# Weight sums on GpSimd, 512-column steps and another order of issue in a fused attention and feed-forward kernel

## The chip, the cores and the metric

The kernel runs on one core of a Trainium2 chip. The metric is the device time of one execution in microseconds. A core has five engines that each run their own instructions in order and wait for each other by semaphores: TensorE (PE in the profile; PEld is its weight load), VectorE (DVE), ScalarE (ACT), GpSimd (POOL) and SyncE (SP), which issues the DMAs here.

## The reference

Four batches of 768 positions with 8 heads of 64 go through chunked attention: each chunk of 32 queries sees 8 memory keys, 16 keys to its left, its own 32 and 8 to its right. The result, 3072 tokens of width 512, goes through a feed-forward layer of width 2048.

```python
for c in range(nc):
    ...
    scores = scale * np.matmul(q_c, k_full.transpose(0, 1, 3, 2))
    scores = scores - np.max(scores, axis=-1, keepdims=True)
    a = np.exp(scores)
    a = a / (np.sum(a, axis=-1, keepdims=True) + 1e-09)
    out[:, :, c_start:c_end] = np.matmul(a, v_full)
...
h = x @ w_in
g = np.where(pos, h, np.where(neg, 0.0, (h + beta) ** 2 / (4.0 * beta)))
return (g @ w_out)
```

## The kernel before, in words

The 3072 tokens are six blocks of 512 (`TB`), each of two halves of 256. The width of 2048 is 16 column groups of 128 (`NFC`), counted by `fc` from 0. Every float32 factor of the feed-forward layer is split into a high part and a low part, and a product is three matmuls: high x high, high x low and low x high.

The program has two parts.

**Blocks 0 and 1.** Generators of small pieces of work are advanced one piece at a time, in the order that the string `FIRST` (line 27) writes out. A name there is one piece, a `+` is the next load of the list `early` (line 811).
- `g0` to `g3` are the attention of block 0 (line 253); `n0`, `n1` are that of block 1's halves, `n2`, `n3` that of block 2 (line 410): scores on PE, softmax on DVE and ACT, six transposes on DVE into `pt`, values on PE, then the high and low parts `xth` and `xtl`.
- `w0` to `w15` decode a piece of the weights (line 189) that a DMA brought as `w`: a scaling on ACT, three bit operations on DVE into `f`, the high part on ACT and the low part on DVE, both into `wr`. Piece i holds the first layer's weights of group i + 1 and the second layer's of group i - 1, but for the ends.
- `A`, `B`, `C`, `D` with a group's number are a `half_step` (line 443) on one half of 256 tokens: `A` and `B` on the halves of block 0, `C` and `D` on those of block 1. It has 12 matmuls of 256 columns into a bank of `ps_h` (two banks), three activations on ACT into `gw` and `gt`, a join on DVE into `gw`, the high part `gh` on ACT, the low part `gl` on DVE, and 6 matmuls of 512 columns into `ps_o`. Two half steps share each of the buffers `gw`, `gt`, `gh`, `gl`.
- `t0` to `t7` are a `build` (line 536), one for every two groups of the first layer's weights. It makes what the second part needs: `fef` is high plus low (two sums of 512 columns), `tf` four differences of 256 columns, all six on DVE. Then ACT casts `tf` into the high half of `st`, DVE makes the low half, and SP stores `st` to DRAM as `saved`. `st` has one buffer; `fef`, `tf`, the decode's `f` and the output's `ob` share two buffers of one tag.

**Blocks 2 to 5.** Here the first layer is computed with seven products in place of eight, on sums of the weights (`saved`, loaded back into freed places of the weights, `load_t`, line 564) and on sums of the tokens. Four strings `QUADS` (line 66) give the order of work within a block, a quarter of the groups each: `p` is a product of 12 matmuls of 256 columns into one of the two `ps_h` banks, `c`, `a`, `r`, `m`, `h`, `l` are the copies, additions, activations, joins and splits behind it, `g` the 12 matmuls of 512 columns of an output, digits and `@` advance the attention of the next block. A `-` means the quarter before. The last pieces of block 1 are left over for the first of these quarters (`left`, line 787, `left_store`, line 792). `begin_second` (line 723) issues the first loads of `saved` on SP.

The class `InOrder` (line 86) keeps every engine's instructions in the order in which the code issues them; its line 94 is the line that the profile shows for nearly all of them.

Of the kernel before, what the change touches and what calls it, by code (L numbers as in the profile page):

```python
# [32 lines left out]
    A4 w10 + A4 B3 w5 B4 A5 w11 w6 + B4 w6 A4 w7 w7 B4 A5 B5 B4 w12 + A5 w6 B4 A5 B5 A5 w7 w13 A6 +
    B5 w7 w8 A5 w8 B5 A6 B6 B5 w14 A6 w7 A6 B5 B6 A6 w8 w15 A7 B6 w8 w9 A6 w9 B6 A7 B6 B7 A7 w8 A7
    B6 B7 A7 w9 A8 B7 w9 w10 w10 A7 B7 A8 B7 B8 A8 w9 A8 B7 A8 B8 w10 A9 B8 w10 w11 w11 B8 A8 A9 B8
    A9 B9 w10 A9 A9 B8 w11 B9 B9 A10 w11 w12 w12 B9 A9 A10 B9 w11 B10 A10 w12 A10 B9 B10 A10 w12
    w13 A11 B10 w13 B10 A10 A11 B10 w12 n0 A11 w13 A11 B11 + n0 w13 B10 A11 B11 n0 A12 B11 n0 w13
    B11 A11 A12 n0 B12 n0 n0 B11 n0 B11 B12 A12 n0 A12 A13 A12 n0 n0 A12 A13 w14 n0 B13 w14 n0 A14
# [10 lines left out]
    C11 D12 C10 n3 n3 C11 C12 n3 n3 D12 C12 D12 n3 n3 D12 + C11 n3 D13 n3 C11 D11 D13 C11 n3 D12 n3
    C12 D12 C12 D13 D13 D13 n3 C12 C13 + n3 n3 n3 C13 C12 D14 C13 D14 D13 D14 D14 C14 D14 C13 D15  # L50
    C14 C13 C14 C15 D15 C14 C14 D15 C15 D15 C15 C13 D15 C15 C15
# [48 lines left out]
def attn_ffn_kernel(ctx: ExitStack, tc: tile.TileContext, first_qk, first_v, qk, vw, w, out):  # L100
# [342 lines left out]
    def half_step(blk, half, fc):  # L443
# [41 lines left out]
        ob = apool.tile([P, 2, DM], F32, name="ob", tag="f", bufs=2)  # L485
        for t, copy in enumerate((dve.tensor_copy, act.copy)):
            copy(ob[:, t], acc[blk][2 * half + t])
            r0 = blk * TB + (2 * half + t) * P
            sp.dma_start(out[r0 : r0 + P, :], ob[:, t])
            yield  # L490
# [448 lines left out]
```

## Time and profile before

| what | value |
| --- | --- |
| median of three runs | 609.87 us (609.29 to 611.09) |
| the profiled execution's own time | 609.82 us |
| its span, first to last instruction | 608.0 us |
| PE busy | 583.4 us, 96% |
| PE weight loads busy | 518.6 us, 85% |
| DVE busy | 402.0 us, 66% |
| ACT busy | 344.8 us, 57% |
| POOL busy | 0.7 us |
| granted TensorE clock, mean | 0.994 |

A busy time is the time in which at least one instruction of the engine runs. A row of a timeline has start, length, engine, line, operation, tiles written and read, and in brackets the idle time ahead of it with what ended it. A row of a group has the number of instructions behind an x, the busy time, the mean of one in ns, and the idle time ahead. The part with 40 slices gives the busy share of each fortieth of the span in tenths.

### The profile page before, as it was taken

The page shows a single profiled execution, that of the slowest core. Times are in us where ns is not written, and L with a number is a line of the kernel's source. Part 1 is how long each engine was busy: PE and PEld are TensorE (multiplying, and loading weights), DVE is VectorE, ACT ScalarE, POOL GpSimd, SP SyncE. Part 2 cuts the span into 40 slices and gives each one's busy share as a digit, 9 for nine tenths or more (in the row PEclk, how much of TensorE's full clock was granted, in tenths as well). Part 3 has the DMA queues.
Part 4 walks back from the last instruction along what each step waited for, and adds up shares of the span by engine and source line. Part 5 has one row for each costly group of instructions (what it writes and reads, how often), then busy time and mean ns, then how long its engine had stood idle before and what let it go on. Part 6 is the DMA issues. An engine that isn't in the chain of part 4 may idle for free.

```text
span 608.0 us, 14641 instructions
## 1 busy us (share of the span) xinstructions
PE 583.4 (96%) x6360; PEld 518.6 (85%) x6360; DVE 402.0 (66%) x643; ACT 344.8 (57%) x683; POOL 0.7 (0%) x6
## 2 busy tenths in 40 slices
...
DVE  5799999997899575755557655556655557423332
...
GB/s 354 423 418 419 15 1 106 85 109 192 138 140 248 237 79 237 208 164 150 139 72 114 199 124 189 140 71 106 208 110 101 138 2 5 204 104 46 130 1 70
DMA packets 39441, 91.13 MB, mean 150 GB/s; under 512 B 2896, under 2 KB 29776, under 8 KB 33744
## 3 DMA queue, kind: packets, MB, share of 16 engines
...
q10 hardware_dynamic: 144, 0.13, 0.1%
q14 instruction: 15, 0.12, 0.1%
...
## 4 chain that ended last, share of the span: by engine, by line
PE 74%; DVE 20%; issue 2%; ACT 2%; DMA 1%; DVEq 0%
PE ps_o L94 36%; PE ps_h L94 32%; DVE f L94 5%; PE ps_x L94 3%; PE ps_s L94 2%; DVE pt L94 2%; DVE wr L94 2%; DVE gw L94 2%; DVE pr L94 2%; DVE gl L94 2%; DVE den L94 1%; DVE st L94 1%; DVE mx L94 1%; DVE tf L94 1%; DMA qk<-in_first_qk_dram 1%
## 5 line engine op out<-in xcount | busy, mean ns | idle before, releaser
L94 PE MATMUL ps_o<-wr,gh 128*128 128x512 f32 x768 | 242.3, 397 | 2.0 <-DVE ob L94 1.6
L94 PEld LDWEIGHTS ps_o<-wr,gh 128*128 128x128 f32 x768 | 137.9, 189 | 28.7 <-DVE ob L94 2.4
L94 PE MATMUL ps_o<-wr,gl 128*128 128x512 f32 x384 | 151.6, 395 | 0.1
L94 PE MATMUL ps_h<-xth,wr 128*128 128x256 f32 x512 | 104.4, 291 | 5.5 <-ACT gt L94 5.2
L94 PE MATMUL ps_h<-s,wr 128*128 128x256 f32 x768 | 98.1, 282 | 0.0
L94 PEld LDWEIGHTS ps_h<-s,wr 128*128 128x128 f32 x768 | 95.5, 188 | 1.9
L94 PEld LDWEIGHTS ps_h<-xth,wr 128*128 128x128 f32 x512 | 85.3, 195 | 8.5 <-ACT gt L94 5.8
L94 ACT CAST gh<-gw 128x256 fp32r<-128x256 f32 (+1 forms) x128 | 65.1, 514 | 46.1 <-DVE gw L94 46.1
L94 DVE SCALAR_TENSOR_TENSOR gw<-gw,gt 128x256 f32<-128x256 f32 (+1 forms) x112 | 59.6, 535 | 43.5 <-ACT gw L94 43.0
L94 PEld LDWEIGHTS ps_o<-wr,gl 128*128 128x128 f32 x384 | 72.3, 188 | 17.8 <-DVE gl L94 1.0
L94 DVE TENSOR_TENSOR gl<-gw,gh 128x256 fp32r<-128x256 f32 (+1 forms) x128 | 70.2, 553 | 14.7 <-ACT gh L94 13.3
L94 PE MATMUL ps_h<-xtl,wr 128*128 128x256 f32 x256 | 66.3, 289 | 0.6 <-DVE xtl L94 0.6
L94 ACT ACTIVATE gw<-gw 128x256 f32<-128x256 f32 (+1 forms) x128 | 66.6, 521 | 0.0
L94 DVE TENSOR_TENSOR gt<-gt,ps_h 128x512 f32<-128x512 f32 x32 | 21.9, 686 | 53.9 <-ACT gt L94 43.2
L94 PEld LDWEIGHTS ps_h<-xtl,wr 128*128 128x128 f32 x256 | 50.2, 196 | 2.5 <-DVE xtl L94 0.8
L94 ACT ACTIVATE gw<-ps_h 128x256 f32<-128x256 f32 (+1 forms) x80 | 34.1, 426 | 31.5 <-PE ps_h L94 29.4
L94 PEld LDWEIGHTS ps_h<-sa,wr 128*128 128x128 f32 x384 | 47.9, 188 | 1.4
L94 PE MATMUL ps_h<-sa,wr 128*128 128x256 f32 x384 | 48.8, 282 | 0.0
L94 ACT ACTIVATE gw<-gt 128x512 f32<-128x512 f32 x32 | 20.3, 633 | 46.4 <-DVE gt L94 46.4
L94 DVE STREAM_TRANSPOSE pt<-pr 32x512 f32<-32x512 f32 (+1 forms) x60 | 41.6, 700 | 1.3
L94 DVE SCALAR_TENSOR_TENSOR f<-w,f 128x1024 uint32<-128x1024 uint32 x32 | 39.1, 1221 | 0.4
L94 ACT COPY gt<-ps_h 128x512 f32<-128x512 f32 x32 | 18.8, 587 | 35.2 <-PE ps_h L94 34.8
...
## 6 DMA issues: line engine op xcount, KB each, us to landing
...
w<-in_w_dram SPq DMA_DIRECT2D x16, 1024.0 KB, 19.8
...
v<-in_vw_dram SPq DMA_DIRECT2D x10, 1024.0 KB, 5.6
saved<-st SPq DMA_DIRECT2D x8, 1024.0 KB, 3.9
...
```

The source lines that it names most:

```text
L94: return self.tc.keep_in_program_order(getattr(self.engine, name)(*args, **kwargs))
```

## The change

Three things change.

1. A new generator `step` takes the place of two half steps from the fifth column group on (`fc` 4 to 15), in both blocks: `E` for block 0, `F` for block 1. It works on 512 tokens at once: 12 matmuls of 512 columns into `ps_h`, and one instruction of 512 columns where two half steps had one of 256 each. The 12 matmuls of the second layer are issued in two pieces of 6. Groups 0 to 3 stay half steps.
2. The six sums of a `build` are issued on GpSimd instead of VectorE. The cast on ACT, the low half on DVE and the store stay.
3. `FIRST` and the four strings `QUADS` are written in another order. What is left over for the second part are now the ends of `F14` and `F15`; it is the same number of matmuls.

```diff
-    + g0 w0 g1 w1 g2 + g2 g1 g0 g3 g2 + g1 g2 A0 + g3 g3 g2 g2 g3 g2 A1 A0 + g3 w2 g3 g3 g3 g2 w1
+    + g0 w0 g1 w1 g2 + g2 g1 g0 g3 g2 + g1 g2 A0 + g3 g2 g2 g3 g2 g3 A1 A0 + g2 g2 + g3 g3 w1 A1 w2
...
-LAST = 4
...
-                pe.matmul(to, a[:, ts], m, start=fc == 0 and i == 0, stop=fc == NFC - 1 and i == 2)
+                pe.matmul(to, a[:, ts], m, start=fc == 0 and i == 0, stop=False)
...
+    def step(blk, fc):
+
+        xh, xl = xts[blk]
+        hp = ps_h.tile([P, 512], F32, name="ps_h")
+        wh, wl = weights(0, fc, 0), weights(0, fc, 1)
+        terms = [(wh, x, cc) for cc in range(NP) for x in (xh, xl)] + [(wl, xh, cc) for cc in range(NP)]
+        for i, (m, x, cc) in enumerate(terms):
+            pe.matmul(hp, m[:, cc * P : (cc + 1) * P], x[:, cc], start=i == 0, stop=i == len(terms) - 1)
+        yield
+        g = gpool.tile([P, TB], F32, name="gw", tag="gw")
+        t = gpool.tile([P, TB], F32, name="gt")
+        act.activation(g, hp, AF.Relu, bias=0.5, scale=0.5)
+        act.activation(t, hp, AF.Relu, bias=-1.0)
+        act.activation(g, g, AF.Square)
+        yield
+        dve.scalar_tensor_tensor(g, g, 1.0, t, op0=ALU.min, op1=ALU.add)
+        yield
+        gh = gpool.tile([P, TB], F32R, name="gh", bufs=4)
+        act.copy(gh, g)
+        yield
+        gl = gpool.tile([P, TB], F32R, name="gl", bufs=4)
+        dve.tensor_tensor(gl, g, gh.bitcast(F32), op=ALU.subtract)
+        yield
+        wh, wl = weights(1, fc, 0), weights(1, fc, 1)
+        for half in range(2):
+            for t in range(2 * half, 2 * half + 2):
+                ts = slice(t * P, (t + 1) * P)
+                for i, (a, m) in enumerate(((gh, wh), (gh, wl), (gl, wh))):
+                    pe.matmul(acc[blk][t], a[:, ts], m, start=False, stop=fc == NFC - 1 and i == 2)
+            yield
...
-            dve.tensor_tensor(fef[:, j].rearrange("p a b -> p (a b)"), hi, lo, op=ALU.add)
+            pool.tensor_tensor(fef[:, j].rearrange("p a b -> p (a b)"), hi, lo, op=ALU.add)
...
-        dve.tensor_tensor(tf[:, 1], b12, b11, op=ALU.subtract)
+        pool.tensor_tensor(tf[:, 1], b12, b11, op=ALU.subtract)
...
     def left(which):
-        two = {"22": (0, 2), "21": (2, 4), "12": (4, 4)}[which]
-        for blk, half, fc in items[len(items) - LAST :][slice(*two)]:
-            next(chains[f"{'ABCD'[2 * blk + half]}{fc}"], None)
+        for name in {"22": (2, 2), "21": (1, 1), "12": ()}[which]:
+            next(chains[f"F{NFC - name}"], None)
...
+        "E": lambda fc: step(0, fc),
+        "F": lambda fc: step(1, fc),
```

**Where the sums stood.** The first place is the end of block 1's weight builds. On DVE before, the sums `fef` and `tf` stand between the softmax of an attention (`den`, `rin`, `pr`) and the low parts `gl` and `st`:

```order
L94 TENSOR_TENSOR st<-tf,st 128x4x256
L94 TENSOR_TENSOR fef<-wr_1173 128x512
L94 TENSOR_REDUCE den<-pr 128x16
L94 TENSOR_TENSOR tf<-fef 128x256 x2
L94 TENSOR_TENSOR tf<-fef,tf 128x256
L94 TENSOR_SCALAR den<-den 128x16
L94 TENSOR_TENSOR gl<-gw,gh 128x256
L94 TENSOR_TENSOR tf<-fef,tf 128x256
L94 RECIPROCAL rin<-den 128x16
L94 TENSOR_TENSOR fef<-wr_1295 128x512
L94 TENSOR_TENSOR pr<-pr,rin 128x1024
L94 TENSOR_TENSOR st<-tf,st 128x4x256
```

The same stretch on DVE now, from one low half `st` to the next:

```order
L89 TENSOR_TENSOR st<-tf,st 128x4x256
L89 TENSOR_TENSOR pr<-ps_s,mx 128x1024
L89 TENSOR_TENSOR gl<-gw,gh 128x512
L89 SCALAR_TENSOR_TENSOR gw<-gw,gt 128x512
L89 TENSOR_REDUCE den<-pr 128x16
L89 TENSOR_TENSOR st<-tf,st 128x4x256
```

And POOL now, where nothing but the sums of one build after the other stands there (the sixth and the seventh):

```order
L89 TENSOR_TENSOR fef<-wr_907 128x512
L89 TENSOR_TENSOR fef<-wr_958 128x512
L89 TENSOR_TENSOR tf<-fef 128x256 x2
L89 TENSOR_TENSOR tf<-fef,tf 128x256 x2
L89 TENSOR_TENSOR fef<-wr_978 128x512
L89 TENSOR_TENSOR fef<-wr_1042 128x512
```

The sums have moved from DVE to POOL, and DVE's rows for the activations are 512 columns wide in place of 256.

**What ACT does between two casts into `st`.** The second place is ACT at the same builds. Before, from the sixth cast to the seventh and the activations behind it:

```order
L94 CAST st<-tf 128x4x256
L94 CAST gh<-gw 128x256
L94 ACTIVATE pr<-pr 128x1024
L94 CAST gh<-gw 128x256
L94 CAST st<-tf 128x4x256
L94 ACTIVATE gw<-ps_h 128x256
L94 ACTIVATE gt<-ps_h 128x256
L94 ACTIVATE gw<-gw 128x256
```

Now, from the sixth cast to the seventh and the activations behind it:

```order
L89 CAST st<-tf 128x4x256
L89 ACTIVATE gw<-ps_h 128x512
L89 ACTIVATE gt<-ps_h 128x512
L89 ACTIVATE gw<-gw 128x512
L89 CAST gh<-gw 128x512
L89 CAST st<-tf 128x4x256
L89 ACTIVATE gw<-ps_h 128x512
L89 ACTIVATE gt<-ps_h 128x512
L89 ACTIVATE gw<-gw 128x512
```

A whole step's activations, which read a `ps_h` bank, have come between the two casts; before there was none.

**The decode beside the attention.** The third place is DVE in block 0, where the first attention half of block 1 (`pr`, `pt`) meets the decode of the 15th piece of weights (`w_847` before, `w_814` now). Before:

```order
L94 TENSOR_TENSOR pr<-pr,rin 128x1024
L94 SCALAR_TENSOR_TENSOR gw<-gw,gt 128x256
L94 STREAM_TRANSPOSE pt<-pr 128x512
L94 TENSOR_TENSOR gl<-gw,gh 128x256
L94 STREAM_TRANSPOSE pt<-pr 128x512
L94 STREAM_TRANSPOSE pt<-pr 32x512
L94 TENSOR_SCALAR f<-w_847 128x1024
L94 STREAM_TRANSPOSE pt<-pr 32x512
L94 SCALAR_TENSOR_TENSOR f<-w_847,f 128x1024
L94 STREAM_TRANSPOSE pt<-pr 32x512 x2
L94 SCALAR_TENSOR_TENSOR gw<-gw,gt 128x256
L94 SCALAR_TENSOR_TENSOR f<-w_847,f 128x1024
```

Now:

```order
L89 TENSOR_TENSOR pr<-pr,rin 128x1024
L89 STREAM_TRANSPOSE pt<-pr 128x512 x2
L89 STREAM_TRANSPOSE pt<-pr 32x512 x4
L89 SCALAR_TENSOR_TENSOR f<-w_814,f 128x1024
L89 TENSOR_SCALAR f<-w_859 128x1024
L89 SCALAR_TENSOR_TENSOR gw<-gw,gt 128x512
L89 SCALAR_TENSOR_TENSOR f<-w_814,f 128x1024
L89 TENSOR_TENSOR xtl<-ps_x,xth 128x4x2x64
L89 SCALAR_TENSOR_TENSOR f<-w_859,f 128x1024
L89 TENSOR_TENSOR xtl<-ps_x,xth 128x4x2x64
L89 TENSOR_TENSOR gl<-gw,gh 128x512
L89 TENSOR_TENSOR wr_1322<-f,wr_1322 128x1024
```

The six transposes now stand in one row, ahead of the two combining operations on the 15th piece, and the decode of the 16th piece (`w_859`) has begun among them.

More of the change, by code (lines that the diff above doesn't have):

```diff
@@ L33 @@
[L33 to L38, printed above, removed]
@@ L49 @@
[L49 to L51 removed]
+    + g0 w0 g1 w1 g2 + g2 g1 g0 g3 g2 + g1 g2 A0 + g3 g2 g2 g3 g2 g3 A1 A0 + g2 g2 + g3 g3 w1 A1 w2
+    g3 w1 w3 A0 g3 g2 w2 g3 + g3 w1 w2 g2 + g3 g3 g2 A0 g3 B0 w1 w2 w1 w4 A0 B0 w3 A1 B0 w2 + A2 B1
+    A1 A2 B1 w2 A1 w3 A0 B1 B2 + w5 w3 B1 A2 B0 B0 B2 B1 w3 w4 A3 B2 + w3 A2 w7 A2 w4 B0 w5 A1 B2
@@ new lines @@
+    A2 w6 w4 w5 B3 A3 B2 w4 + B1 B2 w4 E4 + A3 B3 + w8 w6 + w9 A3 w5 w5 A3 w6 w10 B3 w11 w6 w5 w7
+    B3 A3 + E4 + w6 B3 E5 E4 E5 E4 w13 w7 B3 w6 w7 E4 w8 w7 w12 + E6 E5 E4 E4 E7 E5 w8 w14 + E6 E5
+    E5 E5 w7 w15 w8 w9 E6 w8 w9 E6 E6 E7 w9 E6 E7 w8 w9 E6 w9 E7 E7 E8 w10 E8 E9 w11 w10 w10 E8 w10
+    E8 w11 E9 E7 E8 w11 w10 w11 E8 E9 E9 E8 w12 w12 w11 E9 E10 E10 E11 w12 E7 w13 E10 w12 E10 w13 +
+    n0 E10 + E11 w12 E12 E10 E12 E10 n0 w14 w13 w13 n0 E11 n0 E9 w13 E9 E11 n0 E11 n0 E11 n0 n0 +
@@ new lines @@
+    n0 E13 n0 n0 n0 n0 E11 n0 w14 n0 E13 w15 E12 n0 w14 n0 w15 E12 n0 E14 E12 w14 E14 n1 w14 w15
+    E12 w15 n1 E15 E13 n1 E14 E13 n1 E14 E13 n1 C0 E12 n1 w15 n1 E14 n1 C0 n1 n1 n1 E15 E13 n1 C1
+    E15 E13 n1 E15 E14 C1 n1 E15 C1 C2 + C0 C2 C0 C2 C1 n1 C1 E14 n1 C0 n1 E15 n1 C2 E15 C0 E15 E15
+    D0 E15 C1 D1 C3 E15 t0 D0 t0 t0 t0 D3 D0 D1 t0 C2 C3 D1 D0 D1 t0 t0 t1 D0 C3 D0 C3 t0 C3 t1 t1
+    D2 F4 D1 t1 D3 D2 t1 t1 D3 t1 t2 C2 D1 D2 D2 C3 D3 F5 F4 t2 t2 t2 t1 t2 D2 D2 t2 D3 F6 F4 F4 t2
+    t2 F5 F5 t3 t3 t3 F4 t3 t3 F5 D3 F6 F5 F6 F5 t3 t4 F6 t3 t3 t4 F5 t4 F7 t4 n2 t4 F4 t4 t5 t5 F7
@@ L52 @@
+    F4 t4 F7 n2 F6 t5 t5 t4 n2 F8 F7 t5 F7 F9 t5 F8 n2 F8 F6 t6 n2 t6 t6 t5 t6 F6 F9 F8 F7 t5 t6 F8
+    F9 n2 t6 t7 F7 n2 + n2 n2 F11 n2 t6 t7 t6 t7 n2 t7 t7 n2 F10 n2 F11 F9 F9 n2 F10 t7 F10 F12 t7
+    F8 n2 t7 + n2 F10 F8 F10 F11 F11 n3 F13 n3 F9 n2 n3 F12 F10 n3 F11 F12 + F10 n3 n3 F12 F9 n3 n2
+    n3 n3 F11 F13 n3 n3 n3 F12 F11 F14 F13 F14 n3 F12 F12 F13 n3 n3 F15 n3 + F14 F13 n3 F15 F15 F15
+    F13 F15 F14 F14 F13 n3
 """
-LAST = 4
 PROD = {
@@ L67 @@
     """
-    @S0 p2 p1 c1 -h12 -l12 -g22 a11 0 dS4 r11 p6 c2 m11 0 p5 h11 -g12 kS4 0 p7 z0 -g21 0 c3 a22 r22
-    0 z1 l11 0 m22 h22 p3 p4 r21 a12 r12 l22 m21 m12 g11 h21 l21
-    """,
-    """
-    0 0 -h12 p1 p2 0 c1 -g21 0 -l12 a11 0 r11 m11 -g22 p6 c2 h11 0 p5 p7 0 @V0 c3 a22 r22 0 -g12
-    m22 h22 p4 l11 p3 a12 r21 l22 @S1 m21 r12 m12 h21 l21 g11
-    """,
-    """
-    p1 -h12 1 p2 c1 1 a11 r11 1 -l12 m11 -g21 -g22 p6 1 c2 p5 1 p7 c3 a22 h11 -g12 r22 m22 l11 1 p4
-    h22 l22 r21 1 p3 g11 m21 h21 1 a12 1 1 l21 r12 m12 1
-    """,
-    """
-    -g22 p1 1 -h12 c1 p2 -l12 p6 a11 r11 1 kA11 m11 -g21 @V1 c2 1 p7 h11 kA12 l11 dS3 c3 p5 a22
-    -g12 dS1 r22 dS2 p4 p3 m22 h22 g11 l22 a12 r21 kA22 r12 m21 h21 m12 kS1 l21 kS2 kS3
+    @S0 p1 p2 -h12 -g22 c1 p6 a11 p5 0 dS4 r11 0 m11 -l12 0 -g12 c2 kS4 p7 -g21 c3 0 a22 r22 z0 h11
+    z1 0 0 m22 h22 l11 p4 p3 r21 0 a12 l22 r12 g11 m21 h21 l21 m12
+    """,
+    """
+    0 p2 -h12 0 p1 c1 a11 -g21 p6 -l12 r11 m11 0 0 c2 h11 -g22 p7 p5 0 0 c3 a22 @V0 r22 -g12 p4 p3
+    0 m22 h22 l22 l11 r21 a12 r12 @S1 g11 m21 h21 l21 m12
+    """,
+    """
+    1 1 p2 p1 -g22 c1 a11 r11 1 p6 m11 1 1 -h12 p5 -g21 c2 p7 -l12 c3 h11 -g12 a22 l11 r22 m22 1 1
+    h22 p4 l22 r21 p3 1 g11 m21 h21 1 a12 r12 m12 1 1 l21
+    """,
+    """
+    p1 1 -h12 -g22 c1 p2 p6 -g21 a11 c2 -l12 1 kA11 @V1 r11 p7 1 c3 m11 h11 kA12 p5 dS3 a22 -g12
+    dS1 r22 dS2 p4 p3 l11 m22 h22 l22 kA22 a12 r21 g11 m21 r12 kS2 kS1 h21 m12 l21 kS3
     """,
@@ L483, in half_step @@
         if fc < NFC - 1:
             return
[L485 to L490, printed above, removed]
+        for half in range(2):
+            ob = apool.tile([P, 2, DM], F32, name="ob", tag="f", bufs=2)
+            for t, copy in enumerate((dve.tensor_copy, act.copy)):
+                copy(ob[:, t], acc[blk][2 * half + t])
+                r0 = blk * TB + (2 * half + t) * P
+                sp.dma_start(out[r0 : r0 + P, :], ob[:, t])
+                yield
```

23 lines of the change are left out of this document (5 added, 18 removed).

## The prediction

> **What bounds the kernel now.** I read the page first, then busy time by stretch, then the engines' timelines where TensorE (PE) stands idle. The page:
>
> ```profile
> span 608.0 us, 14641 instructions
> PE 583.4 (96%) x6360; PEld 518.6 (85%) x6360; DVE 402.0 (66%) x643; ACT 344.8 (57%) x683; POOL 0.7 (0%) x6
> ...
> DVE  5799999997899575755557655556655557423332
> ```
>
> PE is busy 96% of the span, VectorE (DVE) only 66%, but DVE's row reads 9 through most of the first third. A busy PE may still be a waiting one, so the next view is busy time by stretch:
>
> ```profile
> 38.00:55.00 17.00, 17.00 (x110) 15.44 (x109) 16.82 (x26) 15.45 (x33) 0.00 (x0) 1.00 1.01 420
> 55.00:110.00 55.00, 55.00 (x473) 49.85 (x472) 54.48 (x80) 39.41 (x90) 0.00 (x0) 1.00 0.20 77
> 110.00:135.00 25.00, 24.09 (x477) 21.07 (x475) 24.07 (x41) 13.30 (x34) 0.00 (x0) 1.00 0.32 107
> 135.00:180.00 45.00, 44.81 (x438) 40.39 (x431) 37.06 (x78) 26.17 (x69) 0.00 (x0) 1.00 0.42 165
> 180.00:191.00 11.00, 6.03 (x33) 5.42 (x33) 10.98 (x20) 4.80 (x11) 0.00 (x0) 0.85 0.37 149
> 191.00:236.00 45.00, 43.35 (x731) 38.01 (x733) 29.92 (x58) 23.67 (x65) 0.00 (x0) 1.00 0.59 199
> 236.00:596.00 360.00, 360.00 (x3547) 323.00 (x3532) 199.33 (x298) 202.51 (x354) 0.00 (x0) 1.00 0.39 120
> ```
>
> The columns are length, PE, weight loads, DVE, ACT, POOL, granted clock, DMA share and rate. From 38 us on PE idles 0.91 + 0.19 + 4.97 + 1.65 = 7.7 us, none of it after 236. The clock of 0.85 over 11 us takes 1.65 us more. So 9.4 us is all that better waiting can give after 38 us. Whether PE is also at its pace is read from the chain of waits, where pieces stand end to end:
>
> ```profile
> 242.11 4.29 PE ps_h L94 x36
> ...
> 257.69 5.57 PE ps_o L94 x24
> ```
>
> A 256-column matmul takes 4.29/36 = 119.2 ns, a 512-column one 5.57/24 = 232.1 ns; two halves cost 238.4. PE is the bound from 38 us on, with one hole of 5 us. DVE is full at the same time from 38 to 135, and keeps up by little: the 15th piece of weights is split at 114.28 + 1.22 = 115.50 and first used at 116.36.
>
> ```profile
> 114.28 1.22 DVE L94 TENSOR_TENSOR wr<-f,wr 128x1024 fp32r<-128x1024 f32 x1
> ...
> 116.36 0.64 PE L94 MATMUL ps_o<-wr,gh 128*128 128x512 f32 x2
> ```
>
> The hole, in ScalarE's (ACT's) timeline and PE's:
>
> ```profile
> 179.43 1.05 ACT L94 CAST st<-tf 128x1024 fp32r<-128x1024 f32 x1 [2.64 <-DVE fef L94]
> ...
> 186.37 1.04 ACT L94 CAST st<-tf 128x1024 fp32r<-128x1024 f32 x1 [4.33 <-DMA saved<-st]
> 187.32 0.38 ACT L94 ACTIVATE gw<-ps_h 128x256 f32<-128x256 f32 x1
> ...
> 188.02 0.58 PE L94 MATMUL ps_h<-xth,wr 128*128 128x256 f32 x1 [4.97 <-ACT gt L94]
> ```
>
> ACT is in order. The sixth cast into st came after 2.64 us of waiting for DVE's sums. The seventh cast (st has one buffer) waited 4.33 us for the store of the build before; the activations that free a ps_h bank stood behind it, and PE behind them.
>
> **The change part by part.** *Columns.* 12 steps in each of two blocks, 12 first-layer matmuls each: 288 of 512 columns for 576 of 256, 288 x (238.4 - 232.1) ns = 1.8 us, on PE's path. The 512-column row writes ps_o; into ps_h the price is not shown. Bounds: 0 (it costs two halves) and 2.3 us. DVE and ACT save in the same steps; DVE's rows:
>
> ```profile
> L94 DVE TENSOR_TENSOR gl<-gw,gh 128x512 fp32r<-128x512 f32 x64 | 44.0, 688 | 9.2 <-ACT gh L94 8.2
> L94 DVE SCALAR_TENSOR_TENSOR gw<-gw,gt 128x512 f32<-128x512 f32 x48 | 32.9, 686 | 37.7 <-ACT gw L94 37.7
> L94 DVE SCALAR_TENSOR_TENSOR gw<-gw,gt 128x256 f32<-128x256 f32 x64 | 26.7, 421 | 5.8 <-ACT gw L94 5.3
> L94 DVE TENSOR_TENSOR gl<-gw,gh 128x256 fp32r<-128x256 f32 x64 | 26.2, 418 | 5.5 <-ACT gh L94 5.1
> L94 DVE TENSOR_TENSOR fef<-wr 128x512 f32<-128x512 f32 x16 | 10.7, 681 | 0.1
> L94 DVE TENSOR_TENSOR st<-tf,st 128x1024 fp32r<-128x1024 f32 x8 | 9.8, 1223 | 2.5 <-ACT st L94 2.4
> L94 DVE TENSOR_TENSOR tf<-fef,tf 128x256 f32<-128x256 f32 x16 | 6.7, 421 | 0.1
> L94 DVE TENSOR_TENSOR tf<-fef 128x256 f32<-128x256 f32 x16 | 6.3, 418 | 0.9 <-DMA out_dram<-ob 0.8
> ```
>
> Two halves cost 2 x (421 + 418) = 1678 ns, a step 688 + 686 = 1374: 0.30 us each, 3.6 us in the first block. Not on the path by itself, because PE sets the pace; it is slack for what follows.
>
> *Sums to POOL.* Eight builds leave DVE with 10.7 + 6.7 + 6.3 = 23.7 us, in the stretch around the hole, where DVE was full. ACT's cast and DVE's split of st stay. What a sum costs on POOL no row shows. POOL's own nearest rows:
>
> ```profile
> masks.py:199 POOL TENSOR_SCALAR_AFFINE_SELECT ident<-ident 128x128 f32<-128x128 f32 x1 | 0.3, 294 | 0.1
> masks.py:197 POOL MEMSET ident<- 128x128 f32 x1 | 0.2, 205 | 0.3 <-POOLq L925 0.3
> ```
>
> The select takes 294 ns for 128 columns with one input: 1.18 us for 512, 0.59 for 256, a build of 2 + 4 operations 2 x 1.18 + 4 x 0.59 = 4.7 us. Lower bound: DVE's own 23.7/8 = 3.0 us. Upper bound: twice the select for two inputs, 9.4 us. I take 4.7, from the row on the engine itself. The Trainium skill, GPSIMD Engine Reference, section 3.1, gives 4497 ns for a sum of 2048 columns; my estimate by that page is 1.1 and 0.56 us, 4.5 us a build, and the total would not move.
>
> How much time a build has:
>
> ```profile
> L94 ACT CAST st<-tf x8: 1045/1052/1062, 145.5 to 194.4; 128x1024 fp32r<-128x1024 f32 x8
> ```
>
> and how long the store of one takes to land, from the page's DMA issues:
>
> ```profile
> saved<-st SPq DMA_DIRECT2D x8, 1024.0 KB, 3.9
> ```
>
> Eight casts in 194.4 - 145.5 us are 7.0 us apart. Counting PE's rows between the eight stores in both orders at the two prices, before had gaps of 0.8 (the sixth to the seventh: the hole) to 7.3, and now 6.0 to 8.1. One turn of st takes 1.05 (cast) + 1.22 (split) + 3.9 (store) = 6.2 us: it fits every gap but the smallest, which it misses by 0.2. tf has one more turn, sums 4 x 0.59 + 1.05 + 1.22 = 4.6 us, which fits. So the hole goes: 4.97 + 1.65 = 6.6 us. The new wait is ACT's cast for POOL; the next step's activations are queued behind it, and PE behind these for a ps_h bank. At 4.7 of 7.0 us the sums are ready before; I put 0.5 us for the close places, between 0 and 4.
>
> *Order in the first block.* DVE's order puts all six transposes of an attention ahead of the last shifts of the 15th piece. Counted at the row prices, that piece's split stands 0.7 us later in DVE's work and its first use 1.6 us earlier in PE's: of the 0.9 us in hand, 1.4 is missing. The transposes of the second attention half, counted the same way, are 2.2 us late where before they were 0.6. The lateness is one delay, not a sum: 2.2 - 0.6 = 1.6 us more, with bounds 0 (PE runs behind its order) and 3. The start up to 38 us is the same work for DMA, DVE and ACT: nothing.
>
> *Rest.* The second part's four tables only permute; PE was never idle there and each bank's reader has at least one output group (2.78 us) between: 0, bounds 0 and +2. SP's loads of saved sums at its start now have 13 instead of 18.6 us of PE work to the first use; a 4.2 us load behind a 1 MB value load (5.6 us) still fits. The other 2.75 us of idle time I leave as it is; it could also go.
>
> *Sum*, against the profiled execution of 609.82 us (span 608.0 plus 1.8 around it; the median of the three runs is 609.87): 609.82 - 1.8 - 6.6 + 1.6 + 0.5 = 603.5 us.
>
> **The rivals.** *POOL is too slow (slower).* If two inputs double the select's price, a build takes 9.4 us against 7.0. ACT's cast then holds the activations back in every build, and PE with them: 8 x 2.4 = 19 us, and without the 0.5 us allowed above 603.0 + 19 = 622 us. It decides from 7.0 us a build. For it: no row shows POOL with two inputs. Against: 128 columns of memset take 205 ns, so much of a POOL operation is fixed, and the select's scaling is already too dear.
>
> *DVE and POOL exclude each other.* A step is 24 x 232.1 ns = 5.6 us of PE, so in 7.0 us DVE has 7.0/5.6 = 1.26 steps of 1374 ns and one split of 1.22, 2.95 us of operations with both inputs in SBUF. If none of these may run beside a POOL sum, 2.95 + 4.7 = 7.65 us must fit into 7.0: 8 x 0.65 = 5.2 us late, 603.0 + 5.2 = 608.2 us. The profile of before says nothing on it, since POOL is idle throughout. The Trainium skill, SBUF — State Buffer, "Who interferes with whom", says that a DVE instruction with two SBUF inputs contends with GpSimd reads and that the second to issue is blocked in full; by that page this change pays for what it moves. No run here shows it yet.
>
> *The order loses elsewhere.* A wait of some 4.5 us that the counts miss, in the first block where DVE stays full (a lateness of 3 instead of 1.6 and POOL waits of 3.6): 608 us.
>
> **How the numbers follow.** Forecast 0.60 (own range 599.5 to 606.5), POOL too slow 0.12, exclusion 0.15, loss elsewhere 0.13. The likeliest time is 603.5 us. The low end takes 2.3 for the columns, all 9.4 of idle time and clock, and no lateness, 598.1, which asks for everything at once: 599. The high end takes in exclusion and loss elsewhere with a few us on top, 610; what lies above is the POOL rival and their tails. A measurement of this kernel can tell about 0.3%, 1.8 us: faster is below 608.0, slower above 611.7. Faster 0.60 + 0.06 + 0.07 = 0.73, same 0.07 + 0.04 = 0.11, slower 0.12 + 0.02 + 0.02 = 0.16.
>
> **What would show it.** Right: PE's idle time near the sixth and seventh st casts gone, clock 1.00 there, a POOL sum of 512 columns near 1.2 us, ps_h rows of 512 columns near 232 ns apart, small PE waits for DVE between 100 and 135. Wrong: POOL busy well over 38 us, ACT's st casts waiting for POOL tf, DVE rows of gw and gl above 688 ns while POOL runs, or PE idle time after the first two blocks.

## The result, and the profile after

| kernel | median, us | lowest to highest | runs |
| --- | --- | --- | --- |
| before | 610.18 | 609.29 to 611.09 | 4 |
| after | 606.53 | 606.19 to 606.94 | 4 |

The ratio is 0.994, 95% interval 0.9923 to 0.9958: 0.6% faster. The profiled execution took 606.56 us with a span of 604.8, against 609.82 and 608.0. The forecast of 603.5 was 3 us too low; its range and sign hold. But the experiments show that the total came about in another way than the sum said.

The page after, with the totals, then the slices of POOL:

```profile
span 604.8 us, 13956 instructions
PE 582.8 (96%) x6072; PEld 503.7 (83%) x6072; DVE 388.5 (64%) x547; ACT 332.4 (55%) x587; POOL 55.0 (9%) x54
...
POOL 0000000005899200000000000000000000000000
```

Busy time by stretch (length, PE, weight loads, DVE, ACT, POOL, clock, DMA share, GB/s):

```profile
38.00:55.00 17.00, 17.00 (x97) 15.33 (x97) 15.68 (x24) 14.55 (x30) 0.00 (x0) 0.91 1.02 421
...
110.00:135.00 25.00, 23.52 (x465) 20.26 (x466) 24.03 (x34) 13.22 (x27) 0.00 (x0) 1.00 0.30 108
135.00:180.00 45.00, 43.35 (x333) 35.16 (x332) 27.39 (x30) 22.27 (x46) 35.25 (x32) 1.00 0.36 141
180.00:191.00 11.00, 11.00 (x49) 8.86 (x48) 9.68 (x9) 5.66 (x9) 9.54 (x9) 1.00 0.46 177
191.00:236.00 45.00, 44.30 (x680) 36.04 (x680) 33.43 (x49) 22.63 (x40) 9.52 (x9) 1.00 0.61 216
236.00:592.00 356.00, 355.30 (x3488) 318.39 (x3487) 195.17 (x293) 198.20 (x351) 0.00 (x0) 1.00 0.39 121
```

The hole at 180 to 191 us is gone: idle 0 for 4.97 and clock 1.00 for 0.85. Against that stand idle times that before did not have: 1.65 us (0.19 before) while POOL works between 135 and 180, 0.70 after 236 (0 before), and a clock of 0.91 for 17 us at 38, which is 1.5 us (in the other kernels below with this start it is 0.89 to 0.99 there, in those with the start of before 1.00).

POOL's groups over the span, with mean ns and the idle time ahead:

```profile
L89 POOL TENSOR_TENSOR fef<-wr 128x512 f32<-128x512 f32 x16 | 25.0, 1582 | 140.2 <-DMA out_dram<-ob 139.6
L89 POOL TENSOR_TENSOR tf<-fef,tf 128x256 f32<-128x256 f32 x16 | 15.9, 995 | 0.6
L89 POOL TENSOR_TENSOR tf<-fef 128x256 f32<-128x256 f32 x16 | 13.7, 879 | 4.4 <-DVE st L89 4.0
```

A build takes (25.0 + 15.9 + 13.7)/8 = 6.83 us of POOL, where the sum had 4.7. ACT's timeline shows what the casts into st wait for now, and the next fence, PE's timeline, what PE waits for in the same place:

```profile
185.52 1.05 ACT L89 CAST st<-tf 128x1024 fp32r<-128x1024 f32 x1 [1.71 <-POOL tf L89]
...
193.78 1.05 ACT L89 CAST st<-tf 128x1024 fp32r<-128x1024 f32 x1 [5.19 <-POOL tf L89]
...
195.22 0.59 ACT L89 ACTIVATE gt<-ps_h 128x512 f32<-128x512 f32 x1
```

```profile
195.87 0.50 PE L89 MATMUL ps_h<-xth,wr 128*128 128x512 f32 x1 [0.69 <-ACT gt L89]
```

A cast still waits 5.19 us with the activations behind it, longer than the 4.33 us behind the old hole, and PE idles 0.69 us for it. So the hole did not go because the casts no longer wait. What else kept PE busy, and what each part of the change is worth, is what the runs were for.

### The profile page after: what moved, and what is told of

Read it like the earlier page. It is cut to its first block, busy times and chain, and to the rows that moved or that the text cites. A ratio compares the mean times of both kernels' runs of the same rounds, so it can differ in the third digit from the quotient of the medians.

```text
span 604.8 us, 13956 instructions
## 1 busy us (share of the span) xinstructions
PE 582.8 (96%) x6072; PEld 503.7 (83%) x6072; DVE 388.5 (64%) x547; ACT 332.4 (55%) x587; POOL 55.0 (9%) x54
## 4 chain that ended last, share of the span: by engine, by line
PE 83%; DVE 9%; ACT 2%; DMA 2%; POOL 2%; issue 2%; ACTq 0%; DVEq 0%; POOLq 0%
PE ps_o L89 39%; PE ps_h L89 37%; PE ps_x L89 4%; PE ps_s L89 3%; DVE pt L89 1%; DMA saved<-st 1%; POOL tf L89 1%; DVE f L89 1%; DVE gl L89 1%; DVE pr L89 1%; ACT gw L89 1%; DVE st L89 1%; DVE gw L89 1%; DVE den L89 1%; DMA qk<-in_first_qk_dram 1%
## 5 line engine op out<-in xcount | busy, mean ns | idle before, releaser
L89 PE MATMUL ps_h<-xth,wr 128*128 128x512 f32 (+1 forms) x320 | 92.9, 365 | 0.7 <-ACT gt L89 0.7
L89 DVE SCALAR_TENSOR_TENSOR gw<-gw,gt 128x512 f32<-128x512 f32 (+1 forms) x88 | 61.3, 699 | 47.1 <-ACT gw L89 46.5
L89 DVE TENSOR_TENSOR gl<-gw,gh 128x512 fp32r<-128x512 f32 (+1 forms) x104 | 71.3, 694 | 24.4 <-ACT gh L89 24.1
L89 ACT CAST gh<-gw 128x512 fp32r<-128x512 f32 (+1 forms) x104 | 60.4, 586 | 33.6 <-DVE gw L89 33.6
L89 PEld LDWEIGHTS ps_h<-xth,wr 128*128 128x128 f32 x320 | 60.1, 201 | 10.5 <-ACT gt L89 1.1
L89 ACT ACTIVATE gw<-gw 128x512 f32<-128x512 f32 (+1 forms) x104 | 61.5, 591 | 0.0
L89 PE MATMUL ps_h<-xtl,wr 128*128 128x512 f32 (+1 forms) x160 | 56.8, 364 | 0.6 <-DVE xtl L89 0.6
L89 ACT ACTIVATE gw<-ps_h 128x512 f32<-128x512 f32 (+1 forms) x56 | 29.9, 535 | 48.7 <-PE ps_h L89 39.9
L89 POOL TENSOR_TENSOR fef<-wr 128x512 f32<-128x512 f32 x16 | 25.0, 1582 | 140.2 <-DMA out_dram<-ob 139.6
L89 PEld LDWEIGHTS ps_h<-xtl,wr 128*128 128x128 f32 x160 | 32.6, 204 | 5.2 <-DVE xtl L89 0.8
```

What stands on the lines that cost most here:

```text
L89: return self.tc.keep_in_program_order(getattr(self.engine, name)(*args, **kwargs))
```

## The experiments

Theory 1 is the prediction's: the hole went because the sums left DVE, and POOL's price, the start and the second part gave some of it back. Theory 2: the new order took the hole away, and the move to POOL only costs. Every ratio below is to the kernel before on the same chip, with its 95% interval.

**The sums back on DVE, the new order and the 512 columns kept (e1_dve_sums).** In `build`, six times:

```
-            pool.tensor_tensor(fef[:, j]..., hi, lo, op=ALU.add)
+            dve.tensor_tensor(fef[:, j]..., hi, lo, op=ALU.add)
...
-        pool.tensor_tensor(tf[:, 1], b12, b11, op=ALU.subtract)
+        dve.tensor_tensor(tf[:, 1], b12, b11, op=ALU.subtract)
```

> The changed kernel, with the six sums of each of the eight builds issued by VectorE (DVE) again; nine of their places (t1 to t6) move by up to seven steps, because on one in-order engine a sum cannot stand ahead of the split that frees its buffer. Theory 1 (the hole went because the sums left DVE): DVE's 27.4 + 9.7 us of work between 135 and 191 us gets most of the 23.7 us of sums back, some 57 to 61 us in a stretch of 56, so DVE is full, an st cast waits for DVE's sums again and most of the 6.4 us comes back: 610 to 612 us. Theory 2 (the new order, with 6.0 to 8.1 us between the builds, took the hole away, and GpSimd only adds its own slowness of 6.83 us a build and its contention): 604 us, 2.5 below the changed kernel's 606.5.

603.99 us (603.25 to 605.62), ratio 0.991 (0.9893 to 0.9926): Theory 2. (Its interval and the changed kernel's, 0.9923 to 0.9958, still touch at their ends; e12_pool_same_order below parts them.) Its stretch of the hole, then ACT's timeline, then PE's:

```profile
180.00:191.00 11.00, 11.00 (x49) 8.94 (x48) 10.86 (x20) 5.82 (x10) 0.00 (x0) 1.00 0.58 206
```

```profile
184.17 0.62 ACT L88 CAST gh<-gw 128x512 fp32r<-128x512 f32 x1
189.96 1.05 ACT L88 CAST st<-tf 128x1024 fp32r<-128x1024 f32 x1 [5.16 <-DVE pr L88]
```

```profile
181.75 0.62 PE L88 MATMUL ps_o<-wr,gh 128*128 128x512 f32 x2
...
187.33 0.39 PE L88 MATMUL ps_h<-xth,wr 128*128 128x512 f32 x1
...
195.70 0.62 PE L88 MATMUL ps_o<-wr,gh 128*128 128x512 f32 x2
```

DVE is as full between 180 and 191 us as before (10.86 for 10.98 us), a cast waits 5.16 us, and PE is not idle for a moment. From 181.75 to 195.70 us PE has 24 matmuls into ps_o and then 36 into ps_h, with no idle time ahead of any; the first 48 of them, to 192.9 us, need nothing of what stands behind the waiting cast, because ACT has emptied both ps_h banks by 183.8 us. The new order has laid ready work across the place where ACT must wait. In the kernel before, PE's last matmul ahead of the hole begins at 182.66 us, and the cast's wait runs to 186.37:

```profile
182.66 0.40 PE L94 MATMUL ps_o<-wr,gl 128*128 128x512 f32 x1
```

**The sums on POOL alone, in the kernel before (e2_pool_only).** The reverse edit in the old `build`.

> The kernel before, with nothing changed but the engine of the builds' six sums: GpSimd. Theory 1: DVE's full stretch (37.1 + 11.0 of 56 us between 135 and 191) loses up to 23.7 us, the hole goes and the columns, the start and the second part stay as they were: 610.2 - 6.6 + 2.5 for GpSimd's slowness and contention, 605 to 607 us. Theory 2 (the order is needed): the old order leaves 0.8 us of TensorE work between the stores of the sixth and seventh build, and GpSimd takes 6.8 us a build, so an st cast waits some 6 us for GpSimd with the activations behind it: the hole only changes its cause, 610 to 614 us.

614.21 us (613.72 to 614.52), ratio 1.0073 (1.0057 to 1.0089): 0.7% slower than before. The hole is still there, with another cause (ACT's timeline, then PE's):

```profile
191.27 1.04 ACT L94 CAST st<-tf 128x1024 fp32r<-128x1024 f32 x1 [4.56 <-POOL tf L94]
```

```profile
192.92 0.58 PE L94 MATMUL ps_h<-xth,wr 128*128 128x256 f32 x1 [5.74 <-ACT gt L94]
```

The cast waits for POOL where it had waited for the store. With e1_dve_sums, Theory 1 falls: the hole is gone with the sums on DVE in the new order, and it stays with the sums on POOL in the old one.

**The change with halves of 256 columns (e3_halves), and the same with the sums on DVE (e7_order_only).** In `step`, matmuls, activations, casts and DVE's operations run as two halves:

```
-        for i, (m, x, cc) in enumerate(terms):
-            pe.matmul(hp, m[:, cc * P : (cc + 1) * P], x[:, cc], start=i == 0, stop=i == len(terms) - 1)
+        halves = [slice(h * HT, (h + 1) * HT) for h in range(2)]
+        for q in halves:
+            for i, (m, x, cc) in enumerate(terms):
+                pe.matmul(hp[:, q], m[:, cc * P : (cc + 1) * P], x[:, cc, q], start=i == 0, stop=i == len(terms) - 1)
...
```

> The changed kernel, its order and its GpSimd sums kept, but each step of 512 columns does its matmuls into ps_h, its activations, its casts and its VectorE operations as two halves of 256 columns, one behind the other. Theory 1 (the width is worth its matmuls): 288 matmuls of 512 columns at 232 to 235 ns become 576 at 119.2, 0.9 to 1.8 us, with VectorE and ScalarE off the path: 607.5 to 608.5 us. Rival (the width also relieves the other two engines, 0.30 us of VectorE and about as much of ScalarE per step, where they bound): VectorE, full from 38 to 135 us with 12 such steps, falls 3.6 us behind, TensorE waits for it there, and the sum is 610 to 612 us.

> The changed kernel with the sums on VectorE (as in e1_dve_sums) and every step of 512 columns as two halves of 256 (as in e3_halves): of the change only the order is left. If the parts add up, 603.99 + (610.13 - 606.53) = 607.6 us. If VectorE, with the sums and 0.30 us more in each step, is too full for both, the stretch from 135 to 191 us comes back as a hole: 610 to 613 us. If the order is worth nothing by itself: 610 us.

e3_halves: 610.13 us (609.44 to 612.05), ratio 1.0013 (1.0001 to 1.0026). e7_order_only: 606.15 us (605.51 to 607.53), ratio 0.9952 (0.9937 to 0.9968). With e1_dve_sums and the change itself, the new order has now run in all four ways:

| new order, medians in us (ratios) | sums on DVE | sums on POOL | POOL costs |
| --- | --- | --- | --- |
| steps of 512 columns | 603.99 (0.991) | 606.53 (0.994) | 2.5 |
| halves of 256 columns | 606.15 (0.9952) | 610.13 (1.0013) | 4.0 |
| 512 columns are worth | 2.2 | 3.6 | |

The kernels did not all run on one chip. By the ratios the four differences are 1.8, 3.7, 2.6 and 4.5 us: the signs hold, the sizes are good to about 1 us. The order alone, against its own before of 609.46, is worth 3.3 us. (It has the other tables of the second part and the nine moved places in it.) One way through the table is -3.3 - 2.2 + 2.5 = -3.0 us, for -3.65 measured. That this comes near is no test, since each step starts where the one ahead of it ends; the 0.7 between them is the difference of the two medians of before, 610.18 and 609.46. Of the three edits two gain, and the one that the title names first loses. What the table does test is whether width and engine are independent, and they are not: the additive forecast for e7_order_only, 607.6, was 1.5 us too high. The rival of e3_halves (the width also relieves DVE and ACT) fits where POOL slows DVE, 3.6 us for the 0.9 to 1.8 of the matmuls: PE's longest wait for DVE's gl is 2.31 us in e3_halves and 0.90 in the changed kernel.

The wait for st's one buffer has not gone from the new order either. In e7_order_only the seventh cast waits for the store, longer than in the kernel before (4.33 us), and PE is busy throughout (ACT's timeline, then the stretch):

```profile
192.69 1.05 ACT L88 CAST st<-tf 128x1024 fp32r<-128x1024 f32 x1 [5.02 <-DMA saved<-st]
```

```profile
180.00:191.00 11.00, 11.00 (x71) 9.94 (x70) 10.90 (x24) 6.14 (x16) 0.00 (x0) 1.00 0.47 179
```

**The old casts and splits spaced out (e6_spaced).** In the string of the kernel before, only these steps of the builds (and n2's last two) move:

```
-    ... t6 n2 t7 t6 n2 t6 C7 + n2 t7 C8 n2 t7 D9 C9 D8 n2 t7 n2 C8 C8 t7 D9 t7 n2 D9 t7 C8 C6 t7 n2 D10 ...
+    ... t6 n2 t7 n2 C7 + n2 t7 C8 n2 D9 C9 D8 n2 n2 C8 C8 D9 n2 D9 t6 C8 C6 t6 n2 D10 C9 t7 D9 D10 t7 ...
```

> The kernel before, 256 columns, all sums on VectorE, its old order; only the casts and splits of the last two builds, the four difference sums of the last, and the two steps behind them on the same buffer move later, so that the sixth and seventh store stand some 8.5 us of TensorE work apart, where they stood 2.9 by TensorE's rows (0.8 between the waits). Theory 2 narrowed to one place (the hole was the seventh cast waiting for the one st buffer): the 4.97 us of idle time and 1.65 us of clock go, 603 to 605.5 us. Rival (the hole was VectorE's full stretch, whose sums held the sixth cast up by 2.64 us and would hold the later ones too): 608 to 610 us.

611.5 us (610.96 to 611.59), ratio 1.0033 (1.002 to 1.0046): slower, and above both forecasts. ACT's timeline, then DVE's, its rows between 186.56 and 191.21:

```profile
191.66 0.74 ACT L92 CAST gh<-gw 128x256 fp32r<-128x256 f32 x2 [7.85 <-DVE gw L92]
192.31 1.04 ACT L92 CAST st<-tf 128x1024 fp32r<-128x1024 f32 x1
```

```profile
186.56 1.22 DVE L92 TENSOR_TENSOR pr<-pr,rin 128x1024 f32<-128x1024 f32 x1
...
188.46 0.65 DVE L92 TENSOR_TENSOR fef<-wr 128x512 f32<-128x512 f32 x1
189.03 2.15 DVE L92 STREAM_TRANSPOSE pt<-pr 128x512 f32<-128x512 f32 x3
191.21 0.76 DVE L92 SCALAR_TENSOR_TENSOR gw<-gw,gt 128x256 f32<-128x256 f32 x2
```

The seventh cast no longer waits for the store, as meant. At once the next wait takes its place: the join of a step stands in DVE's queue behind the softmax and the transposes of an attention, and ACT waits 7.85 us for it. By these rows the single buffer st was one of two reasons for the hole; the other is that the last two builds and n2's softmax stand together on DVE. Spacing the casts alone does not help; the new order moves the steps of PE, ACT and DVE as a whole.

**What the sums on POOL cost, in parts (e10_fef_pool, e11_tf_pool, e12_pool_same_order).** The order of e1_dve_sums, with the two sums of 512 columns, the four of 256, or all six issued by `pool` (the first pair of lines in e10, the second and its three like in e11, all in e12):

```
-            dve.tensor_tensor(fef[:, j]..., hi, lo, op=ALU.add)
+            pool.tensor_tensor(fef[:, j]..., hi, lo, op=ALU.add)
...
-        dve.tensor_tensor(tf[:, 1], b12, b11, op=ALU.subtract)
+        pool.tensor_tensor(tf[:, 1], b12, b11, op=ALU.subtract)
```

> As e1_dve_sums (603.99 us), with only the two sums of 512 columns of each build on GpSimd (3.1 us a build in the changed kernel), the four of 256 on VectorE. If the loss comes by contention, in proportion to the time GpSimd works beside VectorE (25.0 of 54.6 us): 605.1 us. If it comes from builds of 6.83 us in 7.0: none is that long now, 603.8 to 604.3 us.

> As e1_dve_sums (603.99 us), with only the four sums of 256 columns of each build on GpSimd (3.7 us a build), the two of 512 on VectorE. By contention in proportion (29.6 of 54.6 us): 605.3 us. By waits on builds that are too long for the gaps: 603.8 to 604.3 us.

> As e1_dve_sums, in its own order of issue with the nine moved places, but with all six sums on GpSimd: what the engine alone does. If the 2.5 us between e1_dve_sums and the changed kernel are the engine's: 606.0 to 607.0 us. If they are the moved places': 603.5 to 604.5 us.

605.21 us (604.5 to 607.28), 605.75 (604.34 to 607.57) and 606.51 (604.97 to 609.5); ratios 0.9937 (0.9915 to 0.9959), 0.9938 (0.9914 to 0.9963), 0.9959 (0.9942 to 0.9975). The last is apart from e1_dve_sums (0.9893 to 0.9926), so it is the engine and not the nine moved places. Counted in the profiled executions, the 1500th matmul begins at 134.89 us in the changed kernel and at 134.39 in e1_dve_sums, the 2560th at 236.48 and 233.82: 2.2 of the 2.7 us arise while POOL works. PE's idle time from 135 to 236 us is 2.35 us for 1.08; 0.69 of it is the wait behind POOL's sums shown above, the rest waits for gl of DVE (0.32 and 0.90) and gh of ACT (0.42). The medians of the other two, 605.2 and 605.8, lie where contention in proportion puts them (605.1, 605.3), and above the 603.8 to 604.3 of waits for long builds; but their intervals overlap that of e1_dve_sums, so by time alone this is a leaning. The rows say more. DVE's groups from 135 to 236 us in the changed kernel (the prediction shows the same groups of before; in e1_dve_sums they are within 3 ns of those):

```profile
L89 DVE TENSOR_TENSOR st<-tf,st 128x1024 fp32r<-128x1024 f32 x8 | 11.7, 1459 | 8.2 <-ACT st L89 8.2
L89 DVE SCALAR_TENSOR_TENSOR gw<-gw,gt 128x512 f32<-128x512 f32 x12 | 11.1, 924 | 6.6 <-ACT gw L89 6.6
L89 DVE TENSOR_TENSOR gl<-gw,gh 128x512 fp32r<-128x512 f32 x12 | 10.9, 925 | 2.1 <-ACT gh L89 2.1
L89 DVE TENSOR_TENSOR gl<-gw,gh 128x256 fp32r<-128x256 f32 x8 | 5.3, 693 | 1.4 <-ACT gh L89 1.4
L89 DVE SCALAR_TENSOR_TENSOR gw<-gw,gt 128x256 f32<-128x256 f32 x5 | 4.7, 955 | 4.5 <-ACT gw L89 4.5
```

Same operations, same sizes: 236 to 238 ns more for each of 512 columns and for the split of st, 275 and 534 ns more for each of 256. By counts that is 8 x 0.236 + 12 x 0.238 + 12 x 0.237 + 8 x 0.275 + 5 x 0.534 = 12.5 us. The change takes 23.7 us of sums off DVE, and 12.5 us come back as longer rows. The next run shows how they become longer.

**POOL's reads without POOL in the chain (e8_shadow).** As e1_dve_sums, DVE makes the sums; POOL does sums of the same weights that nobody reads:

```
+        dve.memset(mark, 0.0)
+        pool.tensor_copy(spare[:, 0:4], mark)
...
             dve.tensor_tensor(fef[:, j]..., hi, lo, op=ALU.add)
+            pool.tensor_tensor(spare, hi, lo, op=ALU.add)
...
+        for _ in range(4):
+            pool.tensor_tensor(spare[:, 0:HQ], hi[:, 0:HQ], lo[:, 0:HQ], op=ALU.subtract)
```

> As e1_dve_sums (sums on VectorE, 603.99 us); GpSimd in each build also does two sums of 512 and four of 256 columns of the same weights into a spare buffer, begun by a 4-column mark of VectorE at the build's first sum; nobody waits for them. It has GpSimd's reads and writes without GpSimd in the chain. If the 2.5 us that the sums on GpSimd cost are contention for SBUF: 606 to 607 us, VectorE's rows beside them longer (256 columns above 550 ns for 420). If they are waits for GpSimd's results (6.83 us a build): 604 to 604.5 us.

630.83 us (628.11 to 633.73), ratio 1.035 (1.0325 to 1.0375): far beyond both numbers. POOL's six sums of the first build stand merged in one row. Then come three sums by themselves (the last from the second build), each with the row of DVE that begins beside it, and DVE's first row behind the end of the six:

```profile
140.60 6.78 POOL L88 TENSOR_TENSOR spare<-wr 128x512 f32<-128x512 f32 x6
...
141.97 1.62 POOL L88 TENSOR_TENSOR spare<-wr 128x512 f32<-128x512 f32 x1
142.36 1.78 DVE L88 TENSOR_TENSOR fef<-wr 128x512 f32<-128x512 f32 x1
...
146.58 0.80 POOL L88 TENSOR_TENSOR spare<-wr 128x256 f32<-128x256 f32 x1
146.71 0.95 DVE L88 TENSOR_TENSOR tf<-fef,tf 128x256 f32<-128x256 f32 x1
147.58 0.41 DVE L88 TENSOR_TENSOR gl<-gw,gh 128x256 fp32r<-128x256 f32 x1
...
150.95 1.35 POOL L88 TENSOR_TENSOR spare<-wr 128x512 f32<-128x512 f32 x1
151.08 2.31 DVE L88 TENSOR_TENSOR st<-tf,st 128x1024 fp32r<-128x1024 f32 x1
```

Add start and length: DVE's row ends 0.28 us after POOL's where it has 256 columns (147.66 and 147.38), 0.55 where it has 512 (144.14 and 143.59) and 1.08 where it has 1024 (153.39 and 152.30). Undisturbed these rows take 0.42, 0.69 and 1.22 us. So DVE's row stands still until POOL's sum is done, and then runs but for its first 0.14 us. The same holds in the changed kernel: all 26 rows of DVE with two SBUF inputs that begin when a sum of POOL has more than 0.14 us to go end 0.28, 0.55 or 1.08 us behind that sum, by their size, to within about 0.01 us (44 of 45 such rows here). It holds the other way round too: a sum of POOL in whose time such a row of DVE ends takes about 1.15 us more from there for 512 columns and 0.60 for 256. But for the first parts of their rows, the two engines run one behind the other.

Nobody waits for POOL here, so this is contention and nothing else. From 135 to 236 us PE idles 17.2 us (1.1 in e1_dve_sums), and the granted clock falls to 0.94, 0.78 and 0.89 in the three stretches there (1.00 in e1_dve_sums), another 10 us; together these are nearly all of the 27 us. It is not the changed kernel's 2.5 us: DVE still carries the sums, so more collides. But it shows that the mechanism is enough by itself, and that its price grows steeply where DVE is full.

**The second part's tables as before (e4_old_quads).** `QUADS` of the kernel before in the changed one.

> The changed kernel with the four tables of the second part as they were before. Theory 1 (the new tables cost TensorE the 1.3 us by which the second part got longer, its waits of 0.79, 0.37 and 0.18 us that before did not have): 605.2 us, 0.2% under the changed kernel. Rival (the second part got longer for another reason, the sums' loads or the end of the first part): 606.5 us, no change.

606.58 us (605.66 to 608.02), ratio 0.9952 (0.9936 to 0.9969): the rival, no change. The tables are worth nothing either way, as forecast. The idle time in the second part is of another kind (PE's timeline of the changed kernel):

```profile
273.53 0.51 PE L89 MATMUL ps_o<-wr,gh 128*128 128x512 f32 x1 [0.52 <-issue]
```

All nine kernels with 512-column steps have such idle time at one or two fixed places there (ahead of the 3026th matmul, in six of them also of the 4042nd or 4043rd), 0.7 to 2.5 us in sum, with the old tables too (1.1 and 0.2 us); the five with 256 columns throughout (before, e2, e3, e6, e7) have none there. The second part from 236 us up to the last outputs, in e1_dve_sums and then in e7_order_only:

```profile
236.00:585.00 349.00, 348.18 (x3452) 312.47 (x3452) 189.43 (x287) 193.73 (x343) 0.00 (x0) 1.00 0.38 120
```

```profile
236.00:585.00 349.00, 348.98 (x3454) 313.11 (x3453) 192.11 (x289) 193.45 (x342) 0.00 (x0) 1.00 0.40 124
```

So 0.8 us of what the width gains is lost again there. The profile names no engine that PE waits for; why, stays open.

**The start as before (e5_old_start), and two steps of it (e9_scale_moved).** e5 puts the first 100 steps of the old order ahead of the rest of the new one; e9 moves two scalings on ACT:

```
-    ... A1 A0 + g2 g2 + g3 g3 w1 A1 w2 g3 w1 w3 A0 g3 g2 w2 g3 + g3 w1 ...
+    ... A1 A0 w2 + g2 g2 + g3 g3 w1 A1 g3 w1 A0 g3 g2 w2 g3 + g3 w3 w1 ...
```

> The kernel with the sums on VectorE of the first experiment (e1_dve_sums, 603.99 us), with the first 100 steps of the order, to about 40 us, as the kernel before has them. Theory (the new start lost what before did not: TensorE's losses against its own pace up to 110 us are 7.9 us there and 8.7 in the changed kernel against 5.6 before): 601.5 to 602.5 us. Rival (the start is set by the arrival of the data, DMA being busy 1.01 of the stretch 38 to 55 us, and whatever is lost there shows in VectorE's queue later): 603.5 to 604.5, no change.

> As e1_dve_sums (603.99 us), with two steps of ScalarE moved: the scaling of the third piece of weights ahead of the copy of the third attention group's probabilities (where the kernel before has it), that of the fourth behind the copy of the fourth's. Theory (the 1.67 us that TensorE waits for that copy at 33 us, and the 2.11 us that VectorE waits for the scalings, are lost for good, because both engines are full from there to 135 us): 602.0 to 603.0 us. Rival (the wait only moves: VectorE's queue or the data set the first 40 us): 603.5 to 604.5 us.

e5_old_start: 606.51 us (605.52 to 610.21), ratio 0.9956 (0.9941 to 0.9971), slower than e1_dve_sums. Joining the two orders pairs the half steps of block 0 otherwise (B1 writes the half of a buffer that B2 writes too, so part of block 0's activations is not the reference's), which adds waits of its own, 2.0 us of PE idle time between 38 and 55 us. It says nothing on the start.

e9_scale_moved: 602.47 us (600.98 to 603.97), ratio 0.9887 (0.9866 to 0.9908). The start in three kernels: ACT and PE in the changed one, then PE in the kernel before, then PE in this one:

```profile
29.99 2.18 ACT L89 ACTIVATE w<-w 128x1024 f32<-128x1024 f32 x2
...
32.04 0.59 ACT L89 COPY pt<-ps_h 128x512 f32<-128x512 f32 x1
...
32.69 1.14 PE L89 MATMUL ps_x<-pt,v 64*64 64x32 f32 x64 [1.67 <-ACT pt L89]
```

```profile
31.73 1.13 PE L94 MATMUL ps_x<-pt,v 64*64 64x32 f32 x64 [0.43 <-ACT pt L94]
```

```profile
30.66 1.14 PE L88 MATMUL ps_x<-pt,v 64*64 64x32 f32 x64 [0.67 <-ACT pt L88]
```

Two scalings of 1.1 us stood ahead of the copy that PE waited for. Moved, the wait falls from 1.67 to 0.67 us and the median by 1.5, as the theory had it; the intervals of e9 and e1 overlap (0.9866 to 0.9908, 0.9893 to 0.9926), so the size is a median's, not settled. Against the changed kernel (0.9923 to 0.9958) e9 is clearly faster, by 0.5% or some 3 us: new order, 512 columns, sums on DVE, two steps moved. It is the best of the versions run.

## Why the prediction was right, and where it was wrong

The time came out inside the range and faster, as forecast, but in part by luck: the largest term of the sum came true for another reason than the one given, POOL's price was too low, and the order's was put in the wrong place.

- *The bound*, PE with one hole: right. What can be had lay there; the width, the sums' engine and the order move the time by 2 to 4 us each around it.
- *Columns, -1.8 us*: right in sign and near in size, 2.2 with the sums on DVE and 3.6 on POOL. PE's price is the predicted one (the 36 matmuls of 512 columns into ps_h shown for e1_dve_sums take 195.70 - 187.33 = 8.37 us, 232 ns each); the extra comes from PE's waits for DVE and ACT, and 0.7 to 0.8 us go back in the second part.
- *"One turn of st ... fits every gap ... So the hole goes"*: the hole went, for another reason. The step failed at "fits": casts still wait, 5.19 us for POOL here and 5.02 us for st's store in e7_order_only. The old order's smallest gap, 0.8 us in the prediction, is 2.9 by PE's rows as they were counted again for e6_spaced. And the sums' leaving DVE was listed as relief for the full stretch, but e2_pool_only shows that it does not remove the hole and e1_dve_sums that it isn't needed. What the gaps between builds measure is only one of the two causes (e6_spaced); the gain is the order's, which has ready matmuls lying where ACT must wait.
- *POOL's price, 4.7 us a build*: mis-sized. Measured 6.83, just under the limit of 7.0 that the prediction had worked out. The fastest rows are already dearer than the select's scaling:

```profile
L89 POOL TENSOR_TENSOR fef<-wr x16: 1285/1300/2307, 140.9 to 195.1; 128x512 f32<-128x512 f32 x16
L89 POOL TENSOR_TENSOR tf<-fef x16: 735/796/1186, 143.6 to 198.1; 128x256 f32<-128x256 f32 x16
```

  At the minima a build is 2 x 1.285 + 4 x 0.735 = 5.5 us, an estimate of POOL undisturbed, for 4.7 by the select and 4.5 by the figure cited from the Trainium skill, GPSIMD Engine Reference, section 3.1; the remaining 1.3 us are POOL's waits for DVE's rows. Both were low, and 6.83 lies between them and the rival's 9.4.
- *POOL waits, +0.5 us*: mis-sized. The whole cost of POOL, waits and contention, is 2.5 us here, 4.0 with halves, just inside the bound of 4. This is the term that carries most of the 3 us miss.
- *The rival that DVE and POOL exclude each other*, 608.2 us: its mechanism is what the runs show, its price is half. A row of DVE with two SBUF inputs and a sum of POOL never run at once but for their first parts (e8_shadow). The rival added whole rows, 2.95 us of DVE and 4.7 of POOL. An estimate from the parts that exclude each other: 1.26 steps x 2 rows x 0.55 + 1.08 = 2.5 us of DVE, 2 x 1.15 + 4 x 0.60 = 4.7 us of POOL, 7.2 us in 7.0, so 8 x 0.2 = 1.6 us for the rival's 5.2; measured, waits included, are 2.5. The sum of the prediction has no term for it. The Trainium skill, SBUF — State Buffer, "Who interferes with whom", names the contention of a DVE instruction with two SBUF inputs and GpSimd's reads, and calls the shared port pair an exclusive lock; the trace agrees that the two exclude each other, by the 0.28, 0.55 and 1.08 us at which DVE's rows end behind POOL's.
- *POOL is too slow*, from 7.0 us a build: did not come, by 0.2 us. In the old order, with smaller gaps, a cast waited 4.56 us for POOL although a build took it (49.5 - 0.7)/8 = 6.1 us (e2_pool_only).
- *Order in the first block, +1.6 us, start at 0*: the size was put in the wrong place. Idle time between 110 and 135 us rose by 0.57 (23.52 for 24.09 us busy), but not by DVE's lateness: PE waits 0.43 us for DVE there, no more than the 0.56 of before, and 1.04 us for nothing that the profile names ("issue"). At the start, put at 0, the copy came 1.24 us later for PE (waits of 1.67 and 0.43 us) and the clock ran at 0.91 for 17 us; e9_scale_moved gets some 1.5 us of it back.
- *Second part, 0*: right for the tables (e4_old_quads), but 0.7 us of idle time came with the width (0.7 to 2.5 in the nine kernels that have it).
- *What would show it*: the clock and the idle time came as listed under "right", POOL's busy time, the waits for POOL tf and DVE's longer rows as listed under "wrong". Both lists were met, because the order's gain and POOL's cost came at once.
